# Output stores issued by ScalarE, one value load behind the x transposes, one key load a weight slice later: a linear-attention and SwiGLU kernel on one Trainium2 core

## Chip, cores and metric

The kernel runs on one NeuronCore of one Trainium2 chip. The metric is the device time of one execution in microseconds (us). Before the change the median of 5 runs is 329.17 us (328.5 to 330.03).

## The reference: what is computed

Eight batches, eight heads, 576 tokens, head size 64. Attention is linear (cosFormer): a feature map `phi` doubles the head size, and keys are summed against values once per head, so that no matrix of 576 by 576 arises. The result is normalised (RMS) and goes through a gated FFN of width 1536.

```python
def phi(x, c, s):                       # c, s: cos and sin of pi/2 * pos / 576
    r = np.maximum(x, 0.0)
    return np.concatenate([r * c, r * s], axis=-1)
kv  = np.einsum('bhsf,bhsd->bhfd', phi(k), v)
z   = np.sum(phi(k), axis=2)
x   = np.einsum('bhsf,bhfd->bhsd', phi(q), kv) / (phi(q) @ z + 1e-06)
x   = x.transpose(0, 2, 1, 3).reshape(8 * 576, 512)
xn  = x / np.sqrt(np.mean(x * x, -1, keepdims=True) + 1e-06) * rms_g
g   = xn @ w_gate                       # 512 -> 1536
out = (g * sigmoid(g) * (xn @ w_val)) @ w_out
```

Inputs and output are float32; the matmuls run in bfloat16.

## The kernel before

**Blocks and steps.** The 4608 rows of x are cut into nine blocks of 512. Block b below 8 holds the first 512 tokens of batch b; block 8 holds the last 64 tokens of all batches. A block has twelve gate/value steps n = 0 to 11 (`gval_step`: eight matmuls of 512 columns, a Silu on ScalarE, a product on VectorE, L426, L435, L441), and then four output steps j = 0 to 3 (`out_step`, numbered n = 12 to 15: twelve matmuls of 512 columns into one of two PSUM banks psC, and then `out_store`). Gate and value banks psG and psV are two each, in turn.

**What lies between.** The attention of the next batch is done inside the steps of the running block. A call `at(blk, n, where, f, ...)` puts work into a step; `run` emits it at the places "pe" (ahead of the step's matmuls), "mid", "pre" (ahead of the Silu or of the output copy) or "post" (behind it). So the order on every engine and queue is written out by hand: each engine takes its instructions in the order in which they are emitted, and an instruction that has to wait holds up all that is behind it on its engine. For batch nb, in block nb - 1:

- `k_phi`, `q_phi` (L209 on ScalarE, L211 on VectorE): the feature maps. `v_cast` (L265): values to bfloat16, in a lower and an upper half.
- `kvz_pe` (L282): keys against values; needs `k_phi` and both halves of `v_cast`.
- `nd_pe`, `nd_post`, `x_sq`, `x_norm` (L310, L364, L375, L387): numerator and denominator, division, RMS.
- `x_tr_dma` (L406): a transpose of x by DMA, issued by SyncE (SP), from the tile xn into xnT, which the next block's matmuls read. `q_tr_dma` (L246) does the same for q.

**Loads.** `load_piece` brings k, v and q of batch nb in block nb - 2, in pieces of 288 KB (k, v) or 256 KB (q), and all of them are issued by SP. Batch 3 differs: its k comes in steps 0 to 3 of block 1, its q in 6 to 10, its v in 10 to 13. The weights are loaded by GpSimd at the start, in slices that `weight_dmas` holds in the order gate, value, gate, value and so on: entry 4 is the gate slice and entry 5 the value slice of columns 512 to 768, entry 8 the gate slice of columns 1152 to 1536. The k of batch 1 waits for an entry of that list, and its `k_phi` runs in steps 6 to 10 of block 0.

**Stores.** `out_store` copies a PSUM bank to SBUF (tile osb, four buffers) and issues its store to HBM. In blocks 1 to 8 ScalarE makes the copy and SP issues the store (L456; in block 8 two stores of 64 rows each, L460).

Of the kernel before, what the change touches and what calls it, by code (L numbers as in the profile page):

```python
# [13 lines left out]
SYNC_DEP = mybir.DependencyInfo(mybir.DependencyClass.Sync, mybir.DependencyReason.DATA)  # L14
# [9 lines left out]
def kernel(  # L24
# [11 lines left out]
    nc = tc.nc  # L36
# [27 lines left out]
    V, A, G = nc.vector, nc.scalar, nc.gpsimd  # L64
# [6 lines left out]
    def load_kv(which, b, r0=0, r1=4, j0=0, j1=NJ):  # L71

        key = (which, b)
        if key not in raw:
            raw[key] = (two if which == "k" else one).tile(
                [P, 4, NJ * D], FP32, name=f"r{which}", tag=f"r{which}"
            )
        src = {"k": k, "v": v}[which]
        return nc.sync.dma_start(
            out=raw[key][:, r0:r1, j0 * D : j1 * D],  # L80
            in_=src[b, 2 * r0 : 2 * r1, :, :]
            .rearrange("h s d -> (h s d)")
            .rearrange("(r p n) -> p r n", p=P, n=NJ * D)[:, :, j0 * D : j1 * D],
        )

    def load_q(b, h0=0, h1=8):
        key = ("q", b)
        if key not in raw:
            raw[key] = one.tile([P, H, 4 * D], FP32, name="rq", tag="rq")
        return nc.sync.dma_start(  # L90
            out=raw[key][:, h0:h1, :],
            in_=q[b, h0:h1, 0:512, :].rearrange("h (p j) d -> p h (j d)", j=4),
        )

    def load_q_tail(b):
        t = four.tile([P, 4, D], FP32, name="rqt", tag="rqt")
        raw[("qt", b)] = t
        for g in range(2):
            d = nc.sync.dma_start(
                out=t[64 * g : 64 * g + 64, :, :],  # L100
                in_=q[b, 4 * g : 4 * g + 4, 512:576, :].rearrange("h s d -> s h d"),
            )
        return d
# [9 lines left out]
    def load_q_tokens(b, j0, j1):  # L113
# [45 lines left out]
        out=th[:, 0:NC_], in0=fidx[:, :], scalar1=ang, scalar2=None, op0=ALU.mult  # L159
    )  # L160
    for c0, c1, less in ((4, 5, 64.0), (5, NC_, float(S))):
        nc.vector.tensor_scalar(
            out=th[64:128, c0:c1], in0=fidx[64:128, c0:c1], scalar1=-less, scalar2=ang,
# [3 lines left out]
        out=th[:, NC_ : 2 * NC_], in0=th[:, 0:NC_], scalar1=math.pi / 2.0, scalar2=math.pi,  # L167
# [93 lines left out]
    def copy(eng, o, i):  # L261
        if eng is nc.scalar:
            nc.scalar.copy(out=o, in_=i)  # L263
        else:
            eng.tensor_copy(out=o, in_=i)  # L265
# [185 lines left out]
    def out_store(eng, blk, j, bank):  # L451
        osb = four.tile([P, DM], FP32, name="osb", tag="osb")
        copy(eng, osb[:, :], bank)
        if blk < 8:
            rows = out[blk * S : blk * S + 512, :].rearrange("(p j) m -> p j m", j=4)
            nc.sync.dma_start(out=rows[:, j, :], in_=osb[:, :])  # L456
        else:
            for i in range(2):
                r0 = (2 * j + i) * S + 512
                nc.sync.dma_start(  # L460
                    out=out[r0 : r0 + 64, :], in_=osb[64 * i : 64 * i + 64, :]
                )

# [25 lines left out]
    weight_dmas = []  # L489
# [142 lines left out]
    def none():  # L632
        return {"pe": [], "mid": [], "pre": [], "post": []}
# [3 lines left out]
    def at(blk, n, where, f, *args):  # L637
        slots.setdefault((blk, n), none())[where].append((f, args))
# [3 lines left out]
            f(*args)  # L642

    d = load_kv("k", 1)
    tc.add_manual_dep(d.ins, weight_dmas[4].ins.name, SYNC_DEP, reason="after most weights")
    gate_q = load_q(1)
    tc.add_manual_dep(
        gate_q.ins, weight_dmas[8].ins.name, SYNC_DEP, reason="after the gate weights"
# [7 lines left out]


    for j in range(NJ):
        at(0, 6 + j // 2, "post", k_phi, V, 1, j, 0)
        at(0, 6 + j // 2, "post", k_phi, A, 1, j, 1)  # L660
    at(0, 10, "post", q_phi, V, 1, 0, 0)
    at(0, 11, "post", q_phi, A, 1, 0, 1)

# [1 line left out]
    for nb in range(2, B):  # L665
        b = nb - 1
# [24 lines left out]
        for j in range(4):  # L691
            n = nds[j]
# [12 lines left out]
    for nb in range(3, B):  # L705

        b = nb - 2
        for i, which in enumerate(("k", "v", "q")):
            for p in range(5 if which == "q" else 4):
                n = (0, 10, 6)[i] + p if b == 1 else 5 * i + p  # L710
                at(b + n // 16, n % 16, "post", load_piece, which, nb, p)

    def gval_step(blk, n, bank=None):
# [8 lines left out]
    def out_step(blk, j):  # L722
        n = 12 + j
        run(blk, n, "pe")
        bank = psC[j % 2][:, :]
        for i in range(NNT):
            if i == NNT // 2:
                run(blk, n, "mid")
            out_mm(blk, j, i, bank)
        run(blk, n, "pre")  # L730
        out_store(nc.scalar, blk, j, bank)
        run(blk, n, "post")
# [12 lines left out]
    for n in range(NNT - 2):  # L745
# [15 lines left out]
        if n == 3:  # L761
            d = load_q_tail(0)
# [11 lines left out]
        if n in nd_at:  # L774
            j = nd_at[n]
# [7 lines left out]
    for j in (2, 3):  # L783
        for n in (NNT - 2, NNT - 1):
            out_mm(0, j, n, banks0[j])
    out_store(V, 0, 2, banks0[2])
    out_store(A, 0, 3, banks0[3])
    for j in (0, 1):
        for n in (NNT - 2, NNT - 1):
# [37 lines left out]
    osb = four.tile([P, DM], FP32, name="osb", tag="osb")  # L827
    for (c0, c1), bank in (((0, 384), psC[1]), ((384, 512), psG[0])):
# [6 lines left out]
        for i in range(2):  # L835
            r0 = (6 + i) * S + 512
            (nc.sync if i == 0 else A).dma_start(
                out=out[r0 : r0 + 64, c0:c1], in_=osb[64 * i : 64 * i + 64, c0:c1]
# [31 lines left out]
```

## Time and profile before

| | |
|---|---|
| median of 5 runs | 329.17 us (328.5 to 330.03) |
| the profiled execution's own time | 329.32 us |
| its span, first to last instruction | 327.5 us |
| TensorE (PE) busy | 315.5 us, 96% |
| VectorE (DVE), ScalarE (ACT), GpSimd (POOL) busy | 186.1, 176.8, 32.1 us |
| mean DMA traffic over the span | 165 GB/s |
| output stores issued by SP, 256 KB each | 32, median 2.6 us to landing |

The profile is one execution. It gives for each engine the time that it was busy, the chain of work that ended last, the waits with what ended them, and each instruction with its start and length. PE is matmul and PEld the weight load beside it; SPq and ACTq are the instructions with which SP and ScalarE issue DMAs, and their length is the issue, not the transfer. In a timeline the columns are the start in us, the length in us, engine, source line, operation, out<-in, the shapes and the count; idle time of the engine ahead of it and what ended that stand in square brackets. A matmul's line can be short of a record, so a step of exactly twice the usual one isn't a wait.

### The profile page before, as it was taken

How to read it: one execution, taken by the hardware profiler on the slowest of the kernel's cores; microseconds unless marked ns; L12 is line 12 of the kernel's file. 1: busy time of each engine (PE TensorE's matmuls, PEld its weight loads, DVE VectorE, ACT ScalarE, POOL GpSimd, SP SyncE). 2: the span in 40 equal slices, each digit the busy share in tenths (PEclk: the TensorE clock that was granted, in tenths of full speed). 3: DMA queues.
4: the chain of work that ended last, by engine and by line, in shares of the span. 5: the costliest groups of instructions: out<-in, count | busy, mean ns of one | idle time of the engine just before them, and what ended most of it. 6: DMA issues, size and time to landing. Idle time of an engine off the chain costs nothing.

```text
span 327.5 us, 6404 instructions
## 1 busy us (share of the span) xinstructions
PE 315.5 (96%) x2406; PEld 160.8 (49%) x2441; DVE 186.1 (57%) x412; ACT 176.8 (54%) x366; POOL 32.1 (10%) x67
## 2 busy tenths in 40 slices
PE   6899999999998999999999999999999999999994
PEld 2488465554444444544454445444544444444442
DVE  6775768787755766578257745773577133203310
ACT  6865775965674457645654576556644233223321
POOL 1660112001100100011001100110011000000000
PEclk9999999999999999999999999999999999999999
DMA  7999999899989665975596569957621400020014
GB/s 255 233 191 267 320 185 333 301 171 220 220 212 220 150 188 167 217 208 164 179 223 194 150 196 210 199 167 215 127 46 32 130 32 0 31 99 1 0 34 96
DMA packets 80337, 53.91 MB, mean 165 GB/s; under 512 B 51377, under 2 KB 67761, under 8 KB 80306
## 3 DMA queue, kind: packets, MB, share of 16 engines
q1 hardware_dynamic: 73264, 48.64, 57.8%
q0 software_dynamic: 6880, 4.72, 9.9%
q8 instruction: 19, 0.31, 0.4%
q10 hardware_dynamic: 162, 0.13, 0.1%
q14 instruction: 12, 0.10, 0.1%
HBM read 37.75 MB, written 9.44 MB: 144 GB/s over the span
## 4 chain that ended last, share of the span: by engine, by line
PE 90%; DMA 3%; ACT 2%; DVE 2%; issue 1%; SPq 0%; ACTq 0%; DVEq 0%
PE psC L446 26%; PE psG L426 26%; PE psV L426 26%; PE psA L282 3%; DMA rv<-in_v_dram 3%; PE psA L310 2%; PE psG L446 1%; PE psG L565 1%; PE psV L565 1%; PE psO L565 1%; ACT kpm L209 1%; PE psC L830 1%; PE psV L254 1%; ACT sg L435 0%; PE psA L317 0%
## 5 line engine op out<-in xcount | busy, mean ns | idle before, releaser
L441 DVE TENSOR_TENSOR hT<-psV,sg 128x512 bf16<-128x512 f32 x102 | 70.4, 690 | 95.1 <-PE psV L426 71.2
L435 ACT ACTIVATE sg<-psG 128x512 f32<-128x512 f32 x102 | 60.6, 595 | 65.2 <-PE psG L426 64.0
L426 PE MATMUL psV<-xnT,wv 128*128 128x512 bf16 (+1 forms) x365 | 92.1, 374 | 0.4
L426 PE MATMUL psG<-xnT,wg 128*128 128x512 bf16 (+1 forms) x352 | 90.9, 374 | 0.7
L446 PE MATMUL psC<-wo,hT 128*128 128x512 bf16 x382 | 88.2, 379 | 0.7
L426 PEld LDWEIGHTS <-wv 128*128 128x128 bf16 x416 | 40.7, 98 | 47.4
L446 PEld LDWEIGHTS <-hT 128*128 128x128 bf16 x420 | 40.2, 98 | 46.7
L426 PEld LDWEIGHTS <-wg 128*128 128x128 bf16 x416 | 38.5, 98 | 41.0 <-DVE xnT L265 0.4
L263 ACT COPY osb<-psC 128x512 f32<-128x512 f32 (+1 forms) x33 | 19.2, 582 | 40.2 <-PE psC L446 38.9
L380 POOL TENSOR_TENSOR rs<-ms,mhalf 128x1 f32<-128x1 f32 x36 | 19.9, 552 | 200.7 <-ACT scr L375 200.7
L387 DVE SCALAR_TENSOR_TENSOR xn<-xt,rs,gb 128x512 bf16<-128x512 f32 x36 | 26.8, 746 | 17.1 <-POOL rs L380 17.1
L375 ACT ACTIVATE scr<-xt 128x513 bf16<-128x513 f32 x36 | 22.8, 634 | 22.6 <-DVE xt L364 22.4
L209 ACT ACTIVATE kpm<-rk,tab 128x256 bf16<-128x256 f32 (+1 forms) x78 | 32.0, 478 | 1.8 <-DMA rk<-in_k_dram 1.8
L364 DVE TENSOR_TENSOR xt<-psA,rec 128x512 f32<-128x512 f32 x35 | 24.2, 691 | 1.2
L211 DVE TENSOR_SCALAR kpm<-rk,tab 128x256 bf16<-128x256 f32 (+1 forms) x84 | 22.3, 329 | 2.3 <-DMA rk<-in_k_dram 2.3
L209 ACT ACTIVATE qp<-rq,tab 128x512 bf16<-128x512 f32 x32 | 22.4, 713 | 0.1
L211 DVE TENSOR_SCALAR qp<-rq,tab 128x512 bf16<-128x512 f32 x32 | 15.4, 494 | 0.4 <-DMA rq<-in_q_dram 0.4
L310 PEld LDWEIGHTS <-qpT 128*128 128x128 bf16 x248 | 11.6, 98 | 6.7 <-issue 0.3
L310 PE MATMUL psA<-kvzs,qpT 128*128 128x65 bf16 x248 | 12.8, 193 | 0.3
L282 PEld LDWEIGHTS <-kpm 64*128 64x128 bf16 x576 | 10.0, 95 | 5.1 <-issue 4.0
L426 PE MATMUL psG<-xnt_tail,wg 128*128 128x512 bf16 x48 | 12.3, 379 | 0.1
L426 PE MATMUL psV<-xnt_tail,wv 128*128 128x512 bf16 x47 | 12.1, 379 | 0.0
(89 smaller groups left out, 166.8 us busy)
## 6 DMA issues: line engine op xcount, KB each, us to landing
out_dram<-osb SPq DMA_DIRECT2D x32, 256.0 KB, 2.6
rv<-in_v_dram SPq DMA_DIRECT2D x21, 288.0 KB, 3.2
rk<-in_k_dram SPq DMA_DIRECT2D x20, 288.0 KB, 3.6
rq<-in_q_dram SPq DMA_DIRECT2D x20, 256.0 KB, 3.2
rk<-in_k_dram SPq DMA_DIRECT2D x2, 1152.0 KB, 8.9
rq<-in_q_dram SPq DMA_DIRECT2D x2, 1024.0 KB, 8.5
rv<-in_v_dram SPq DMA_DIRECT2D x3, 576.0 KB, 8.4
wo<-in_moe_w_out_dram POOLq DMA_DIRECT2D x4, 384.0 KB, 6.9
```

Of the source, the lines that this page charges most:

```text
L209: nc.scalar.activation(out=out_ap, in_=in_ap, func=AF.Relu, scale=scale)
L211: eng.tensor_scalar(out=out_ap, in0=in_ap, scalar1=scale, scalar2=0.0, op0=ALU.mult, op1=ALU.max)
L282: nc.tensor.matmul(banks[c][:, r * E : (r + 1) * E], lhsT=kp_main[b][lo : lo + 64, j, r, :], rhs=vvm[b % 2][lo : lo + 64, r, j, :], start= ...
L310: nc.tensor.matmul(o[:, g, i, :], lhsT=qpT[(b, 0)][:, h, j * P : (j + 1) * P], rhs=kvz_of(b, h), start=True, stop=True,)
L364: nc.vector.tensor_tensor(out=xt[:, 0:DM].rearrange("p (b h d) -> p b h d", b=2, d=D), in0=o[:, :, :, 0:D], in1=rec[:, :, :].unsqueeze(3). ...
L375: nc.scalar.activation(out=scr[:, :], in_=xt[:, 0 : DM + 1], func=AF.Square, scale=1.0 / math.sqrt(DM), accum_out=ms[:, :],)
L380: nc.gpsimd.tensor_tensor(out=rs[:, :], in0=ms[:, :], in1=mhalf[:, :], op=ALU.pow)
L387: nc.vector.scalar_tensor_tensor(out=xn[:, :], in0=x_of[(b, j)][:, 0:DM], scalar=rs_of[(b, j)][:, :], in1=gb[:, :], op0=ALU.mult, op1=ALU. ...
L426: nc.tensor.matmul(pst[bank][:, cols[0] : cols[1]], lhsT=w[:, t, n * P : (n + 1) * P], rhs=x[:, t, cols[0] : cols[1]], start=(t == 0), sto ...
L435: nc.scalar.activation(out=sg[:, :], in_=psG[bank][:, :], func=AF.Silu)
L441: nc.vector.tensor_tensor(out=hTs[blk][:, n, :], in0=psV[bank][:, :], in1=sg[:, :], op=ALU.mult)
L446: nc.tensor.matmul(bank, lhsT=hTs[blk][:, n, j * P : (j + 1) * P], rhs=wo[:, n, :], start=(n == 0), stop=(n == NNT - 1),)
```

## The change

The stores of blocks 1 to 8 are issued by ScalarE in place of SP. All four pieces of v of batch 3 are issued at the end of step 13 of block 1, where the last two x transposes of batch 2 are already emitted, in place of one in each of the steps 10 to 13. The k of batch 1 waits for weight entry 5 in place of 4, and its nine pairs of `k_phi` go from 2, 2, 2, 2, 1 in steps 6 to 10 to 3, 2, 2, 2 in steps 7 to 10.

```diff
@@ out_store
         if blk < 8:
             rows = out[blk * S : blk * S + 512, :].rearrange("(p j) m -> p j m", j=4)
-            nc.sync.dma_start(out=rows[:, j, :], in_=osb[:, :])
+            (nc.scalar if blk else nc.sync).dma_start(out=rows[:, j, :], in_=osb[:, :])
         else:
             for i in range(2):
                 r0 = (2 * j + i) * S + 512
-                nc.sync.dma_start(
+                nc.scalar.dma_start(
                     out=out[r0 : r0 + 64, :], in_=osb[64 * i : 64 * i + 64, :]
                 )
@@ batch 1
     d = load_kv("k", 1)
-    tc.add_manual_dep(d.ins, weight_dmas[4].ins.name, SYNC_DEP, reason="after most weights")
+    tc.add_manual_dep(d.ins, weight_dmas[5].ins.name, SYNC_DEP, reason="after most weights")
...
     for j in range(NJ):
-        at(0, 6 + j // 2, "post", k_phi, V, 1, j, 0)
-        at(0, 6 + j // 2, "post", k_phi, A, 1, j, 1)
+        at(0, 7 + max(0, j - 1) // 2, "post", k_phi, V, 1, j, 0)
+        at(0, 7 + max(0, j - 1) // 2, "post", k_phi, A, 1, j, 1)
@@ load pieces of batches 3 to 7
         for i, which in enumerate(("k", "v", "q")):
             for p in range(5 if which == "q" else 4):
-                n = (0, 10, 6)[i] + p if b == 1 else 5 * i + p
+                n = (p, 13, 6 + p)[i] if b == 1 else 5 * i + p
                 at(b + n // 16, n % 16, "post", load_piece, which, nb, p)
```

## The prediction

> **What bounds the kernel now.** First the page: which engine is full, and what the chain of work that ended last is made of.
>
> ```profile
> PE 315.5 (96%) x2406; PEld 160.8 (49%) x2441; DVE 186.1 (57%) x412; ACT 176.8 (54%) x366; POOL 32.1 (10%) x67
> PE 90%; DMA 3%; ACT 2%; DVE 2%; issue 1%; SPq 0%; ACTq 0%; DVEq 0%
> ```
>
> TensorE sets the time, and SP's queue has no measurable share of the chain. So a change of queues can gain only where PE stands still for a transfer. The list of waits and PE's timeline show where it stands still. From 18.2 us, when the FFN matmuls begin, to 322.7 us there is one such place of over 0.6 us, in block 2, at the keys-against-values of batch 3.
>
> ```profile
> 97.99 0.75 PE L282 MATMUL psA<-vvm,kpm 64*128 64x65 bf16 x36
> 99.97 0.76 PE L282 MATMUL psA<-vvm,kpm 64*128 64x65 bf16 x36 [1.23 <-DVE vvm L265]
> 98.17 0.69 DVE L441 TENSOR_TENSOR hT<-psV,sg 128x512 bf16<-128x512 f32 x1 [0.64 <-PE psV L426]
> 98.77 0.48 DVE L211 TENSOR_SCALAR qp<-rq,tab 128x512 bf16<-128x512 f32 x1
> 99.17 0.76 DVE L265 CAST vvm<-rv 128x1152 bf16<-128x1152 f32 x1
> ```
>
> This looks like a late v, but isn't: the cast of v's upper half follows VectorE's product of step 3 and a q_phi back to back, and the product had to wait for PE itself (0.64). v had landed long before: the last piece was issued at 89.18 us and took 4.0 us, so it was there at 93.2. The 1.2 us is VectorE's written order, which the change leaves alone. The other candidate is the start of block 2 (PE from 90.99 us), which needs the last x transpose of batch 2. SP's timeline, and the landing of the transpose issued at 86.71:
>
> ```profile
> 82.25 1.27 SPq L99 DMA_DIRECT2D rqt<-in_q_dram  x2
> 83.57 0.60 SPq L79 DMA_DIRECT2D rv<-in_v_dram  x1
> 84.27 1.23 SPq L406 DMA_TRANSPOSE xnT<-xn  x1
> 85.60 0.54 SPq L456 DMA_DIRECT2D out_dram<-osb  x1
> 86.19 0.41 SPq L79 DMA_DIRECT2D rv<-in_v_dram  x1
> 86.71 1.39 SPq L406 DMA_TRANSPOSE xnT<-xn  x1
> ...
> DMA to landing us min/median/max: 3.8/3.8/3.8
> ```
>
> Store and v pieces stand between the transposes; the last one lands at 86.71 + 3.8 = 90.5, 0.5 us ahead of its need, and PE shows no gap there. All later x transposes land early (block 2: issued at 118.53, landed after 2.5, needed at 126.3).
>
> **What the Trainium skill says.** "DMA: Bandwidth & Descriptors", section "Issuing engines are not separate DMA queues": DMAs from SP and ScalarE run on the same 16 engines, and issuing from both saves only sequencer time. The trace fits, as the chain gives SPq 0%. "Perfetto Trace Analysis", section "DMA Instruction — HWDGE (DVE, Sync)": an issue holds the sequencer while it waits for the lock of a descriptor generator that the sequencers share, generates, and pushes its semaphore; that whole window is in the profile. Before, hardly anything but SP uses it, so no wait for the lock shows here; it is the unknown of this change.
>
> **Part 1: 34 stores from SP to ScalarE** (28 in blocks 1 to 7, 6 halves in block 8). ScalarE's price is visible once, at the end:
>
> ```profile
> 322.73 0.48 ACT L263 COPY osb<-psC 128x384 f32<-128x384 f32 x1 [1.36 <-PE psC L830]
> 323.24 0.55 ACTq L837 DMA_DIRECT2D out_dram<-osb  x1
> 323.83 0.27 ACT L263 COPY osb<-psG 128x128 f32<-128x128 f32 x1 [0.62 <-PE psG L830]
> ```
>
> From the end of one copy to the next instruction it is 0.62 us; the overlap with the next instruction that is lost (0.1) makes it 0.72. Below, it can't be under the 0.33 of SP's shortest store; above, behind one transpose in the generator (1.2) it is 0.7 + 1.2 = 1.9. I take 0.72. In all 34 x 0.72 = 24 us on ScalarE, which is busy 177 of 327.
>
> Is it hidden? Behind each store wait ScalarE's x_sq and k_phi, and, behind the block's last one, the Silu that frees a PSUM bank for PE. The tightest place is the end of block 1:
>
> ```profile
> 88.60 0.59 ACT L263 COPY osb<-psC 128x512 f32<-128x512 f32 x1 [0.67 <-PE psC L446]
> 89.08 1.30 ACT L209 ACTIVATE kpm<-rk,tab 128x256 bf16<-128x256 f32 x3
> 90.29 0.62 ACT L375 ACTIVATE scr<-xt 128x513 bf16<-128x513 f32 x1
> 91.19 0.59 ACT L263 COPY osb<-psC 128x512 f32<-128x512 f32 x1 [0.19 <-PE psC L446]
> 92.05 0.60 ACT L435 ACTIVATE sg<-psG 128x512 f32<-128x512 f32 x1 [0.28 <-PE psG L426]
> ```
>
> The first store of the block fits into the 0.80 in which ScalarE waits for xt. The second's 0.72 meets 0.67 of idle: 0.05 late. The third adds 0.72, less 0.19; the fourth 0.72, less 0.28. So the Silu of step 0 comes about 1.0 late, ends at 93.65, and PE wants its bank again in step 2, at 94.44 (from PE's timeline): 0.8 us to spare. Steps of 1.73 us with Silu and q_phi spaced 0.5 + 0.6 catch up within two steps. In the output steps of blocks 2 to 6, idle times of 0.8 to 1.3 per step absorb more; block 7 has 2.0 per step. In block 8 a copy and two issues take 0.59 + 2 x 0.6 = 1.8 of a step's 2.6; the last two end near 322.6, the next copy is due at 322.73. On the path: 0. If prices are p, the lateness at block 2 is 2p + (p - 0.67) - 0.47, and it reaches PE when it passes 1.8, from p = 0.98.
>
> A store also waits on ScalarE for its copy (its own engine, 0.03 seen above) and for the landing of the eighth DMA before it, as the records hand out eight completion semaphores in turn: for the last store of block 1 that is the first, 8 us older and landed by then. 0.
>
> SP gains: its stores no longer wait for copies ahead of loads and transposes. What was held up there was early or, at 86.71, 0.5 ahead, so nothing on the path.
>
> **Part 2: v of batch 3 behind the transposes.** No instruction more or less; two pieces leave the space ahead of the last two transposes, a third that between, and the four now follow them. The transpose issued at 86.71 goes at about 86.5, when its x_norm (85.72 + 0.75) is done, and lands after about 2.5 to 3 (the x transposes' median is 2.5, against 3.8 and 4.3 here): near 89.3, 1.7 ahead of its need in place of 0.5. No PE time, as none was lost. The v pieces go from 87.8 to 90.2 and, at the 3.3 to 4.5 us seen, land from 91.5 to 94.7. The casts that read them start at 95.71 and 99.17, in VectorE's order: 2 us or more to spare. What follows them on SP is a tail transpose that block 8 needs, and q transposes from 94.2. 0; at worst, should four pieces beside two stores land 2 us later, 0.3.
>
> **Part 3: k of batch 1.** Gate slice 4 was issued at 14.09 and value slice 5 at 14.82; by their landings (7.4 and 8.0 us) they are there at 21.5 and 22.8. So k leaves 1.3 later, and after its 10.3 lands near 33.1 in place of 31.8. Its first k_phi on ScalarE was at 31.96, 0.2 behind the landing:
>
> ```profile
> 31.96 0.90 ACT L209 ACTIVATE kpm<-rk,tab 128x256 bf16<-128x256 f32 x2
> 33.20 0.60 ACT L435 ACTIVATE sg<-psG 128x512 f32<-128x512 f32 x1 [0.34 <-PE psG L426]
> ```
>
> It moves behind the Silu at 33.20, to 33.69: margin 0.6. Three k_phi (1.3) fit before the Silu at 34.92. In step 10 VectorE has one k_phi more (0.3) ahead of q_phi; its product then comes about 0.1 late, against a PE stall of 0.1 that ScalarE sets there. Weights 6 to 9 share the bandwidth with k a little less; no matmul waits for them before. q of batch 1 waits for slice 8 as before, and v follows it on SP; their casts have some 0.8 of margin. GpSimd's next weights wait for q and move with it. 0, between -0.1 and +0.2.
>
> **The sum.** 0 + 0 + 0 against the profiled execution's 329.32 (span 327.5 and 1.8 around it), which lies 0.15 over the median of 329.17. Half a tenth of a per cent may come from the wider margins in executions that lose them; I take 0.2 us off the median: **328.9**. About 0.3% (1.0 us) is what a measurement of this kernel can tell from no change.
>
> **Rivals.**
> *The margins are lost in ordinary executions.* For it: 0.5 us at the transpose and 0.2 at k are thin, and the runs spread over 1.5 us. A transpose that needs the longest landing seen (q's, 5.7) would come 1.9 later and cost PE 1.4; the fix then gives all of it. Against it: the profiled execution was slower than the median without any such stall. Time: 327.9, within 327.4 to 328.2.
> *ScalarE's issues hold up the Silu (slower).* Place: the end of block 1 and the start of block 2. If transposes and stores queue for the generator (1.2 us each, twice in these steps), the price passes 0.98; at p = 1.3 the lateness is 2.8 and PE stops for 1.0, giving 330.2. Should p be 1.3 in every block, blocks 3 to 7 would lose some 0.5 each, and more than 332. Against it: among loads and transposes SP's stores took 0.33 to 0.65.
> *v too late (slower).* From a landing after 95.7 or 99.2 the cast waits and PE's 1.2 grows by as much: 330. Needs 1 to 4 us more than the landings show.
> That the change doesn't do what it says could be so in part 2 alone, if the pieces were still held by something older on SP; nothing there is.
>
> **How the numbers follow.** No change that counts 0.44 (328.2 to 330.1, most likely 328.9); margins 0.36; slower by ScalarE 0.16, by v or k 0.04. The range takes in the margins' case and ScalarE's at 1 us: 327.5 to 330.4. Faster 0.36, same 0.44, slower 0.20.
>
> **What would show it.** Right: ACTq L456 with some 0.5 us each, the last x transpose of batch 2 landing before 90, PE's 1.2 at 99 still there, and no gap of PE at the start of blocks 2 to 8. Wrong: a PE wait on ScalarE's sg or DVE's hT two steps into a block, ACTq lines over 1 us, a cast or k_phi that waits for its DMA, or a span shorter by over 1 us.

## The result, and the profile after

Median of 28 runs: **328.8 us** (328.45 to 332.04). The kernel before, on the same chip: 328.95 us (47 runs, 328.44 to 330.98). The ratio is 0.9995, with a 95% interval of 0.9983 to 1.0007: no change. The lowest times of the two differ by 0.01 us.

The profiled execution of the kernel after took 330.05 us, span 328.3, 0.8 more than the span before. First it has to be seen where that comes from. Page of the kernel after: engines, the granted clock by slices, and the chain.

```profile
PE 317.5 (97%) x2406; PEld 162.3 (49%) x2441; DVE 185.7 (57%) x412; ACT 177.7 (54%) x366; POOL 31.9 (10%) x67
PEclk9799999999999999999999999999999999999999
PE 91%; ACT 3%; DVE 2%; issue 1%; DMA 1%; ACTq 0%; DVEq 0%
```

PE is busy 2.0 us longer with the same 2406 instructions, and the second slice of the clock shows a 7. Windows of 2 us around it, kernel after (start:end, length, then busy time and count of PE, PEld, DVE, ACT, POOL, and at the end the granted clock, DMA share, GB/s):

```profile
8.00:10.00 2.00, 2.00 (x6) 0.51 (x5) 2.00 (x8) 2.00 (x6) 0.23 (x1) 0.83 1.04 375
10.00:12.00 2.00, 2.00 (x23) 1.79 (x23) 1.52 (x3) 1.28 (x3) 2.00 (x3) 0.50 1.17 283
12.00:14.00 2.00, 1.94 (x76) 1.77 (x72) 0.60 (x4) 0.93 (x3) 2.00 (x4) 0.82 1.40 180
```

The middle window of the kernel before:

```profile
10.00:12.00 2.00, 1.72 (x52) 1.44 (x53) 1.76 (x5) 1.60 (x3) 1.04 (x2) 1.00 1.02 289
```

At half the clock PE got through 23 matmuls there in place of 52. No instruction of the change runs this early, and an execution of the unchanged kernel has a like clock and span (b_again below: mean clock 0.993, span 328.1). So spans of single profiles can't be compared here. What can be compared are distances inside the trace. I cut at two PE instructions: the first output matmul of block 0 (L446) and the first FFN matmul of block 2 (L426).

| kernel | start to block 0's output | from there to block 2 | block 2 to the end | mean clock |
|---|---|---|---|---|
| before | 40.77 | 50.22 | 236.5 | 1.000 |
| after | 41.57 | **50.22** | **236.5** | 0.992 |

Behind the opening, the two executions agree to the hundredth of a microsecond up to block 2, and to the tenth after it. The other profiles of this document say the same of the opening: it took 39.95 to 40.77 us in the seven with a mean clock of 0.997 or more, and 41.41 to 43.70 us in the five with 0.993 or less (store3 and k_7 left aside, the one because its clock fell later, the other because its edit stops PE in the opening). Beneath that equality several things moved. PE's timeline of the kernel after, block 2:

```profile
91.79 1.03 PE L426 MATMUL psG<-xnT,wg 128*128 128x512 bf16 x4
...
98.80 0.75 PE L282 MATMUL psA<-vvm,kpm 64*128 64x65 bf16 x36
100.78 0.75 PE L282 MATMUL psA<-vvm,kpm 64*128 64x65 bf16 x36 [1.23 <-DVE vvm L265]
```

All of it is 0.8 later than before, PE's stop of 1.23 included, which stays exactly as long. Now the two queues that the change works on, SP and ScalarE, at the end of block 1:

```profile
84.01 4.46 SPq L406 DMA_TRANSPOSE xnT<-xn  x2
88.52 2.20 SPq L79 DMA_DIRECT2D rv<-in_v_dram  x4
```

```profile
86.94 0.56 ACT L263 COPY osb<-psC 128x512 f32<-128x512 f32 x1
87.53 0.34 ACTq L456 DMA_DIRECT2D out_dram<-osb  x1
87.92 1.31 ACT L209 ACTIVATE kpm<-rk,tab 128x256 bf16<-128x256 f32 x3 [0.42 <-ACT osb L263]
...
92.23 0.56 ACT L263 COPY osb<-psC 128x512 f32<-128x512 f32 x1
92.82 0.34 ACTq L456 DMA_DIRECT2D out_dram<-osb  x1
93.21 0.60 ACT L435 ACTIVATE sg<-psG 128x512 f32<-128x512 f32 x1 [0.41 <-PE psG L426]
```

On SP nothing stands between the two transposes any more, and the four v pieces follow them. On ScalarE each copy is followed by an issue of 0.34. But the last transpose, issued at 87.28, landed after 4.1 us, at 91.34: not sooner than before (3.8), though v was taken out of its way. That is the number to explain. Its view, the landing of that one instruction in the kernel after:

```profile
L406 SPq DMA_TRANSPOSE xnT<-xn x1: 1192/1192/1192, 87.3 to 87.3; - x1
DMA to landing us min/median/max: 4.1/4.1/4.1
```

### The profile page after: what moved, and what is told of

Read it like the earlier page. It is cut to its first block, busy times and chain, and to the rows that moved or that the text cites. A ratio compares the mean times of both kernels' runs of the same rounds, so it can differ in the third digit from the quotient of the medians.

```text
span 328.3 us, 6386 instructions
## 1 busy us (share of the span) xinstructions
PE 317.5 (97%) x2406; PEld 162.3 (49%) x2441; DVE 185.7 (57%) x412; ACT 177.7 (54%) x366; POOL 31.9 (10%) x67
## 4 chain that ended last, share of the span: by engine, by line
PE 91%; ACT 3%; DVE 2%; issue 1%; DMA 1%; ACTq 0%; DVEq 0%
PE psC L446 26%; PE psG L426 26%; PE psV L426 26%; PE psA L282 3%; PE psA L310 2%; PE psG L446 1%; ACT kpm L209 1%; DMA rk<-in_k_dram 1%; PE psG L565 1%; PE psV L565 1%; PE psO L565 1%; PE psV L254 1%; PE psC L830 1%; PE psO L254 1%; ACT sg L435 0%
## 5 line engine op out<-in xcount | busy, mean ns | idle before, releaser
L426 PE MATMUL psV<-xnT,wv 128*128 128x512 bf16 (+1 forms) x365 | 92.1, 374 | 0.4
L426 PE MATMUL psG<-xnT,wg 128*128 128x512 bf16 (+1 forms) x352 | 90.9, 374 | 0.7
L446 PE MATMUL psC<-wo,hT 128*128 128x512 bf16 x382 | 88.2, 379 | 0.7
L426 PEld LDWEIGHTS <-wv 128*128 128x128 bf16 x416 | 40.7, 98 | 47.4
L446 PEld LDWEIGHTS <-hT 128*128 128x128 bf16 x420 | 40.3, 98 | 46.6
L426 PEld LDWEIGHTS <-wg 128*128 128x128 bf16 x416 | 38.5, 98 | 41.0 <-DVE xnT L265 0.4
L263 ACT COPY osb<-psC 128x512 f32<-128x512 f32 (+1 forms) x33 | 19.2, 580 | 32.5 <-PE psC L446 31.1
L426 PE MATMUL psG<-xnt_tail,wg 128*128 128x512 bf16 x48 | 12.3, 379 | 0.1
L426 PE MATMUL psV<-xnt_tail,wv 128*128 128x512 bf16 x47 | 12.1, 379 | 0.0
```

The source lines that it names most:

```text
L426: nc.tensor.matmul(pst[bank][:, cols[0] : cols[1]], lhsT=w[:, t, n * P : (n + 1) * P], rhs=x[:, t, cols[0] : cols[1]], start=(t == 0), sto ...
L446: nc.tensor.matmul(bank, lhsT=hTs[blk][:, n, j * P : (j + 1) * P], rhs=wo[:, n, :], start=(n == 0), stop=(n == NNT - 1),)
```

## The experiments

The theory of the prediction: all three parts are off the critical path. Rivals: two parts with effects of opposite sign cancel; the gain lies in executions that no profile caught. Each kernel is compared with runs of the kernel before on the same chip; "lowest" is the fastest of its runs.

### The parts alone: p_store, p_v, p_k

```diff
p_store, against before:
-            nc.sync.dma_start(out=rows[:, j, :], in_=osb[:, :])
+            (nc.scalar if blk else nc.sync).dma_start(out=rows[:, j, :], in_=osb[:, :])
...   (and L460: nc.scalar)
p_v, against before:
-                n = (0, 10, 6)[i] + p if b == 1 else 5 * i + p
+                n = (p, 13, 6 + p)[i] if b == 1 else 5 * i + p
p_k, against before: weight_dmas[5], and k_phi in steps 7 to 10, as in the change
```

> The kernel before with the stores of blocks 1 to 8 issued by ScalarE, and nothing else. Main theory (a store issue on ScalarE costs 0.5 us and is hidden below 0.98): no change, within 0.3 us of before; the Silu of step 0 of block 2 some 0.3 us late, no gap of PE at the block starts. A theory in which the parts cancel (stores lose what v or k gains): slower by 0.5 us or more. In the trace I expect the last x transpose of batch 2, now beside a store on another queue and not ahead of it, to take 4 us to its landing.

> The kernel before with v of batch 3 in step 13 behind the x transposes, stores still on SP. Main theory: no change, within 0.3 us. If the transposes were slowed by the v pieces, the last one lands within 3 us of its issue (1.5 us ahead of PE's need); if it is the stores that slow it, it stays near 3.8. The theory that thin margins are lost in ordinary runs expects a gain of 0.5 us or more in the median.

> The kernel before with k of batch 1 behind weight entry 5 and its k_phi one step later, and nothing else. Main theory: no change, within 0.3 us; k lands near 32 to 33 us, ahead of its first k_phi on ScalarE by 0.5 us or more. The theory of lost margins expects a gain; a theory in which the later k delays q and v of batch 1 expects a loss of 0.5 us at 41 to 46 us.

Measured, with 329.94 (lowest 328.54, 51 runs) for before on this chip: p_store 329.63, lowest 328.98, ratio 1.0002 (0.9979 to 1.0024); p_v 329.0, lowest 328.50, 0.9977 (0.9964 to 0.9991); p_k 329.08, lowest 328.52, 0.998 (0.9965 to 0.9995).

The medians hide what the trace of **p_store** shows. PE's timeline has a gap at the start of block 2 that neither before nor after has:

```profile
88.73 5.35 PE L446 MATMUL psC<-wo,hT 128*128 128x512 bf16 x24
94.59 1.02 PE L426 MATMUL psG<-xnT,wg 128*128 128x512 bf16 x4 [0.50 <-DMA xnT<-xn]
```

In **p_v** the stores are still on SP, behind the transpose (SP's timeline, and the landing of the transpose):

```profile
86.10 1.20 SPq L406 DMA_TRANSPOSE xnT<-xn  x1
87.42 0.50 SPq L456 DMA_DIRECT2D out_dram<-osb  x1
87.96 2.20 SPq L79 DMA_DIRECT2D rv<-in_v_dram  x4
```

```profile
L406 SPq DMA_TRANSPOSE xnT<-xn x1: 1195/1195/1195, 86.1 to 86.1; - x1
DMA to landing us min/median/max: 2.4/2.4/2.4
```

2.4 us: about the value that the prediction had taken for the whole change (2.5 to 3). The transpose was there at 88.5, and PE began block 2 at 90.60, a margin of 2.1. So v's move does all that was expected of it only as long as the stores stay on SP. **p_k**: k landed at 32.34, the first k_phi on ScalarE began at 33.12, and nothing waits for it. From block 0's output to block 2, p_v has 50.23 and p_k 50.22, from there to the end 236.5 and 236.6: as before. Their ratios lie 0.2% below one, with intervals that leave one out; taken by the numbers, the margins theory had expected such gains. But no wait of PE is gone in either trace, and the lowest times are those of before. The odd figure is 329.94: in the other comparisons the kernel before had medians of 328.95, 329.22 and 329.27, and kernels that keep both thin margins, at the transpose and at k, had 329.12 and 329.06 on the other chip (b_again and store_not1). So the 0.2% lies more likely in those 51 runs than in the two edits. That isn't shown.

### The stores again, and before against itself: p_store_2, b_again

p_store's profile had a clock of 0.987, so the same kernel was run again beside a second copy of the kernel before.

> The stores of blocks 1 to 8 on ScalarE alone, a second time, for a look at full clock. In the first look the last x transpose of batch 2 took 5.2 us to its landing and PE stopped for 0.7 us at the start of block 2. New theory (on its own queue a store no longer queues behind the transposes but runs beside them and slows them): the gap of 0.4 to 0.7 us is there again, and the time is 0.3 to 0.6 us over before. Old theory (the store is hidden, nothing moves): no gap, the first look was a disturbed one.

> The kernel before, unchanged, against itself: what the comparison shows when nothing differs, and a second look at where its runs differ. Main theory: ratio 1.000, its runs spread over 1.5 us or more, by the granted clock and the first transfers of the opening, with the x transpose of batch 2 in time. The theory of lost margins expects a gap of PE at the start of block 2 in a run at full clock that is a microsecond late.

Measured, with 329.22 (lowest 328.53, 59 runs) for before: p_store_2 330.06, lowest 329.14, 1.0008 (0.9985 to 1.0032); b_again 329.12, lowest 328.50, 0.9996 (0.9979 to 1.0014). p_store_2's profile has a clock of 1.000, and the gap is there (PE's timeline, and the landing of the transpose):

```profile
88.25 2.32 PE L446 MATMUL psC<-wo,hT 128*128 128x512 bf16 x10
90.95 1.02 PE L426 MATMUL psG<-xnT,wg 128*128 128x512 bf16 x4 [0.38 <-DMA xnT<-xn]
```

```profile
L406 SPq DMA_TRANSPOSE xnT<-xn x1: 1188/1188/1188, 85.9 to 85.9; - x1
DMA to landing us min/median/max: 5.0/5.0/5.0
```

From block 0's output to block 2 it is 50.76, 0.54 more than the 50.22 of before (and 0.67 more in p_store's trace); the lowest time is 0.61 up, and was 0.44 up for p_store. The intervals of the ratios are wider than that and take in no change, but two traces and two lowest times say the same, and 14 runs of the kernel before (b_again) have a lowest time that isn't up: **the stores alone cost about half a microsecond.** b_again's trace has 41.41, 50.22 and 236.5 at clock 0.993: the kernel before with the opening of the profile after.

### Where the half microsecond arises: store_not1

```diff
against before:
+            (nc.scalar if blk > 1 else nc.sync).dma_start(out=rows[:, j, :], in_=osb[:, :])
```

> The kernel before with the stores of blocks 2 to 8 on ScalarE, those of block 1 still on SP. If the loss of the stores alone is the two stores of block 1 that run beside the last two x transposes of batch 2, it is gone: no gap of PE at the start of block 2, time as before within 0.2 us, fastest run near 328.5. If the loss is ScalarE's time in every block, some 0.5 us remain.

329.06, lowest 328.63, against 329.27 and 328.62 (47 runs): 1.0004 (0.9975 to 1.0032). The last transpose of batch 2 landed after 3.5 us, block 2 begins without a gap, 50.22 after block 0's output:

```profile
92.10 1.03 PE L426 MATMUL psG<-xnT,wg 128*128 128x512 bf16 x4
```

So 30 of the 34 stores cost nothing that is seen (the lowest time is 0.01 up), and the loss sits in the stores of block 1, which are issued beside the last transposes. The landing of the last x transpose of batch 2, over the kernels:

| stores of block 1 | v pieces | landed after, us | margin to PE, us |
|---|---|---|---|
| SP | behind the transposes (p_v, b_v_cast) | 2.4, 2.4 | 2.1 |
| SP | between (before, b_again, b_cast, store_not1, p_k) | 3.8, 4.0, 3.9, 3.5, 3.5 | 0.45 to 0.9 |
| ScalarE | behind (after, a_cast, k_7, v_late) | 4.1, 4.2, 4.1, 4.2 | 0.3 to 0.46 |
| ScalarE | between (p_store, p_store_2) | 5.1, 5.0 | none, PE waits |

The table has both signs. With the stores on either engine, v's move is worth 0.8 to 1.6 us of landing; with v in either place, the stores' move costs 1.0 to 1.8. On SP the store that becomes ready during the transpose goes out behind it (87.42 in p_v). On ScalarE it goes out at once, 0.25 us after the transpose has started to be issued (87.53 and 87.28 in the kernel after). That the store on ScalarE is what delays the transpose is shown. That it does so by going out earlier, and not by being on another queue, is the reading; no run held a store back on ScalarE. Nor do these runs tell whether the two then share the generation of descriptors or the transfer.

The later blocks, where no v piece stands near, bear the effect out. The last x transpose of batch 5, issued in block 4, has a store 1.30 us behind its own issue on SP in the kernel before, and 0.35 us behind it on ScalarE in the kernel after. The landing, before and then after:

```profile
L406 SPq DMA_TRANSPOSE xnT<-xn x1: 1197/1197/1197, 185.9 to 185.9; - x1
DMA to landing us min/median/max: 2.6/2.6/2.6
```

```profile
L406 SPq DMA_TRANSPOSE xnT<-xn x1: 1190/1190/1190, 186.7 to 186.7; - x1
DMA to landing us min/median/max: 4.3/4.3/4.3
```

It is so with the last x transpose of each of the batches 3 to 7: 2.4 to 2.7 us in the six profiles with these stores on SP, 3.5 to 4.5 us in the seven with them on ScalarE (store3 left aside), store_not1 among them. There the delay costs nothing, because the transpose has time: the one of batch 5 lands at 190.9 in the kernel after, and PE needs it at 194.46. Block 1 is only the place where the margin is thin.

### What does stop PE: a_cast, b_cast, b_v_cast

The one stop of PE, 1.23 us, was read as VectorE's order. The cast of v's upper half goes one step earlier, into step 2:

```diff
a_cast against after; b_cast against before; b_v_cast against before, with p_v's edit as well:
-        at(vb, vn + 1 + (nb == 3), "post", v_cast, V, nb, *HIGH)
+        at(vb, vn + 1, "post", v_cast, V, nb, *HIGH)
```

> The changed kernel with the cast of the upper half of v of batch 3 one step earlier (step 2 of block 2 in place of 3). Main theory: PE's stop of 1.2 us in block 2 is VectorE's written order, so it goes: faster by 1.2 us than before, near 327.7, ratio 0.996. Rival: the stop stands for a late v; then the cast waits for its transfer on VectorE, the products behind it are late, and the time stays at before's within 0.3 us. The last piece of v landed 1.5 us ahead of where the cast would now start.

> The kernel before with the cast of the upper half of v of batch 3 in step 2 of block 2 in place of 3, and nothing else. Main theory (PE's stop of 1.2 us is VectorE's written order, and v is there anyway): faster by 1.2 us, ratio 0.996. If the new place of the v loads is what makes the earlier cast pay, this one stays within 0.3 us of before.

> The kernel before with v of batch 3 in step 13 and its upper cast in step 2, stores still on SP and k as before. Main theory: 1.2 us faster than before (ratio 0.996), as fast as the same cast in the changed kernel, so that neither the stores on ScalarE nor the later k are needed; the last x transpose lands within 3 us. If stores on ScalarE have a worth of their own, it stays 0.3 us or more behind that kernel.

| kernel | median | lowest | ratio to before | before: median, lowest |
|---|---|---|---|---|
| a_cast | 327.46 | 327.13 | 0.9914 (0.9889 to 0.994) | 329.94, 328.54 |
| b_cast | 328.48 | 327.07 | 0.9967 (0.9951 to 0.9984) | 329.22, 328.53 |
| b_v_cast | **327.52** | 327.10 | 0.9945 (0.9929 to 0.9961) | 329.22, 328.53 |

The lowest times are 1.4 us down in all three. VectorE's and PE's timelines of b_v_cast, where the two groups of 36 matmuls have become one of 72 with no wait:

```profile
96.61 0.48 DVE L211 TENSOR_SCALAR qp<-rq,tab 128x512 bf16<-128x512 f32 x1
97.00 0.75 DVE L265 CAST vvm<-rv 128x1152 bf16<-128x1152 f32 x1
97.73 0.69 DVE L441 TENSOR_TENSOR hT<-psV,sg 128x512 bf16<-128x512 f32 x1
```

```profile
97.55 1.33 PE L282 MATMUL psA<-vvm,kpm 64*128 64x65 bf16 x72
```

The cast no longer stands behind the product that waits for PE. From block 2 to the end it is 235.15 us in place of 236.5, so the gain lies behind the start of block 2, where this was PE's only stop of its size. b_v_cast beats both the kernel before and the kernel after. That it beats b_cast isn't shown: their intervals overlap, and the lowest times are equal. a_cast, which has the stores on ScalarE and the later k as well, is no faster (its ratio is taken against the high median of 329.94), so neither of these two is needed.

### ScalarE's price pushed up: store3

Here each store of 512 columns becomes three, on ScalarE, to find the point from which ScalarE's issues reach PE.

```diff
against after:
-            (nc.scalar if blk else nc.sync).dma_start(out=rows[:, j, :], in_=osb[:, :])
+            if blk:
+                for c0, c1 in ((0, 192), (192, 384), (384, 512)):
+                    nc.scalar.dma_start(out=rows[:, j, c0:c1], in_=osb[:, c0:c1])
+            else:
+                nc.sync.dma_start(out=rows[:, j, :], in_=osb[:, :])
```

> The changed kernel with each store of blocks 1 to 7 cut into three by columns (192, 192, 128), all on ScalarE: the issue's price goes from 0.5 to about 1.25 us. By the prediction's sum (2p + (p - 0.67) - 0.47 late, PE stops past 1.8) block 2 starts 0.8 us late, and blocks 3 to 6 by 0.5 to 0.7 each: slower by about 3 us (2 to 5), with waits for sg two steps into a block. If ScalarE goes on while an issue is under way, nothing moves: within 0.3 us of the changed kernel.

348.23 us (346.8 to 348.99, four runs), ratio 1.0562 (1.0529 to 1.0594): 19 us, far more than expected. ScalarE's and PE's timelines, block 1 into 2:

```profile
87.03 1.71 ACTq L458 DMA_DIRECT2D out_dram<-osb  x3
88.78 1.30 ACT L209 ACTIVATE kpm<-rk,tab 128x256 bf16<-128x256 f32 x3 [1.79 <-issue]
90.00 0.56 ACT L263 COPY osb<-psC 128x512 f32<-128x512 f32 x1
91.50 1.62 ACTq L458 DMA_DIRECT2D out_dram<-osb  x3
93.17 1.31 ACT L209 ACTIVATE kpm<-rk,tab 128x256 bf16<-128x256 f32 x3 [2.61 <-DMA rv<-in_v_dram]
...
97.59 1.18 PE L426 MATMUL psG<-xnT,wg 128*128 128x512 bf16 x4 [2.52 <-ACT sg L435]
98.57 1.91 PE L426 MATMUL psV<-xnT,wv 128*128 128x512 bf16 x4
100.27 1.76 PE L426 MATMUL psG<-xnT,wg 128*128 128x512 bf16 x4
```

The place is the one that the prediction named for its slower rival: PE waits for the Silu's bank in step 2. The price is not 1.25. Three issues hold ScalarE 1.3 to 1.8 us, and at least six of them first wait for older DMAs. The prediction had named that wait and put it at nothing: eight completion semaphores go in turn over the DMAs of SP and ScalarE together, so each DMA waits for the eighth before it. With three times the stores, the eighth before it is young. The first issue of the second group could go at 90.6 and went at 91.50, when the x transpose of 86.77 had landed (91.42); the second went at 92.30, when the v piece of 88.02 had landed (92.28). In the kernel after, none of ScalarE's stores waits so. PE stops by 2.7, 2.0, 3.7, 3.2 and 2.9 us in step 2 of blocks 2 to 6 (from start to start of two matmuls, less the usual 0.216; the view's 2.52 is the idle time), and after three of these stops, as here, about seven matmuls run at 0.43 us spacing in place of 0.216. That is 14.5 and some 3 x 7 x 0.21 = 4.4, against the 19.2 by which the part from block 2 to the end is longer (255.7 in place of 236.5). So there is a limit, made of the issues and of the eight semaphores together, and one store per step is well inside it.

### k and v pushed on: k_7, v_late

```diff
k_7 against after:
-    tc.add_manual_dep(d.ins, weight_dmas[5].ins.name, SYNC_DEP, reason="after most weights")
+    tc.add_manual_dep(d.ins, weight_dmas[7].ins.name, SYNC_DEP, reason="after most weights")
v_late against after:
-                n = (p, 13, 6 + p)[i] if b == 1 else 5 * i + p
+                n = (p, 15, 6 + p)[i] if b == 1 else 5 * i + p
```

> The changed kernel with k of batch 1 behind weight entry 7 in place of 5. k leaves near 26 and lands near 35 to 36, past its first k_phi (33.7 to 34.5). ScalarE and VectorE wait for it 1 to 2 us; PE has 1.8 us of room, so no change or up to 0.5 us slower. A loss of over 1 us would say that the margin at k is the tight one.

> The changed kernel with v of batch 3 in step 15 of block 1 in place of 13. Issued some 4 us later, the pieces land near 97 to 100; the lower cast is due at 95.7 to 96.5, the upper at 99.2 to 100. The prediction's threshold says that VectorE then waits for its transfer and PE's 1.2 us at keys-against-values grow by 1 to 3 us: slower by 1.5 us. If VectorE's order alone sets that stop, nothing moves.

**k_7**: 330.81, lowest 329.62, against 329.27 and 328.62: 1.0037 (1.0018 to 1.0055), +1.0 in the lowest, more than expected. ScalarE's and PE's timelines:

```profile
36.28 1.30 ACT L209 ACTIVATE kpm<-rk,tab 128x256 bf16<-128x256 f32 x3 [3.26 <-DMA rk<-in_k_dram]
37.49 0.57 ACT L435 ACTIVATE sg<-psG 128x512 f32<-128x512 f32 x1
38.12 1.02 PE L426 MATMUL psG<-xnT,wg 128*128 128x512 bf16 x4 [1.41 <-ACT sg L435]
```

k left at 26.88 and landed at 36.26; ScalarE stood 3.26 for it, with a Silu behind the k_phi. The Silu came 3.35 later than its place in the rhythm of the steps, PE 1.58 late: 1.8 us are swallowed. That is the room the prediction read from PE's timeline for block 2 (two PSUM banks, a step of 1.73), here confirmed in block 0.

**v_late** tells nothing about v. SP issues nothing in steps 14 and 15 that v could fall behind, so every engine's order is that of the kernel after, and the run is a repeat of it: 328.97, lowest 328.54, 0.9985 (0.9968 to 1.0001). From which lateness v would hurt was not tried.

## Why the prediction was right, and where not

The number was right (328.9 forecast, 328.8 measured), and so was the sum for the whole change: nothing on the path. In part that was luck: of the three zeros, the stores' was wrong by half a microsecond, and v's move, which alone brings the last transpose to 2.4 us, made up for it at the same place. The steps:

- **PE's one stop is VectorE's order: right.** 1.23 before, 1.23 after, gone with the cast one step earlier.
- **ScalarE's price, 0.72 a store: too high.** In blocks 1 to 7 the issue is 0.34 to 0.40, the idle ahead of the next instruction, issue included, 0.42; with the lost overlap of 0.1, some 0.5. (The halves of block 8 take 0.47 to 0.61 each, where 0.6 was said.) Taken back to the time of before, the Silu of block 2's step 0 starts at 92.41 (93.21 - 0.80) against 92.05, so 0.36 late, where 1.0 was worked out; with 0.5 the prediction's formula gives the same 0.36. Either price is inside the 1.8 of room. One reading beside it was off: the third output steps of blocks 2 and 4 have 0.19 of idle on ScalarE, not 0.8 to 1.3. No harm came of it.
- **A wait for a generator shared with SP**, which the Trainium skill describes ("Perfetto Trace Analysis", section "DMA Instruction — HWDGE (DVE, Sync)") and the slower rival needed: not seen in the kernel after. ScalarE's issue at 87.53 lies wholly inside SP's transpose of 87.28 to 88.47, and took 0.34. In store3 it can't be ruled out: the second and third issues of a store took mostly 0.44 to 0.46 where SP issued nothing, and mostly 0.50 to 0.67 beside an issue of SP.
- **"On the path: 0" for the stores: this step failed.** It priced the stores where they went, on ScalarE, and looked at SP only for what gets shorter. It did not ask what the stores' place on SP had been good for: there they were behind the transpose. Alone they cost 0.5, through the last x transpose. The skill's sentence that issuing from two engines saves only sequencer time ("DMA: Bandwidth & Descriptors", section "Issuing engines are not separate DMA queues") was read as "and costs nothing", and SPq 0% in the chain as agreement. The runs of p_store refute that reading, not the section, which says in the same place that DMAs from several engines interleave.
- **The transpose lands after 2.5 to 3, margin 1.7: wrong for the whole change** (4.1, margin 0.46), right for v's part alone (2.4, margin 2.1). The issue time was right: 86.48 in the time of before, where 86.5 was said. By the prediction's own list this was a sign that it didn't bear out: a landing before 90, where it was 90.54 in that time. The zero came out because the two errors meet at this transpose.
- **v: right in effect, landing mis-sized.** The pieces took 5.4 to 6.5 us, not 3.3 to 4.5; the last was there at 96.78, and its cast began at 99.97. The lower half had 1.8 to spare.
- **k: right.** It landed at 32.16, 2.3 ahead of ScalarE's first k_phi at 34.49 (33.1 and 33.69 were forecast). It left at 21.72, 0.25 later than in the profile before, and 1.0 later in p_k, where 1.3 was said. PE shows no wait for the gate and value weights.
- **The margins rival** explained the spread of the runs by lost margins. The traces don't bear it out: what differs between executions of one kernel, as far as profiles caught it, lies in the opening. b_again's profile, 0.8 us over the median of its runs at a clock of 0.993, has the transpose in time. The theory isn't excluded for executions that no profile caught, and p_v's 0.2% could be its remainder.

## What to carry to other kernels

A DMA queue is also an order. Whoever moves a transfer to another engine's queue should list what it stood behind there, for that will now run beside it: here a store of 256 KB that had waited behind a transpose cost it 1.0 to 1.8 us of landing, and PE half a microsecond in the one place where the margin was thinner than that. Where a large rearrangement measures as zero, run its parts alone, and compare distances between two instructions inside the traces rather than spans. And when PE waits for a cast, look first at what stands ahead of the cast on its own engine: one line moved there gave more than all transfers together.

## What was not expected of the hardware

- In the profile after, the granted clock went down to 0.50 from 10 to 12 us, and to 0.83 and 0.82 beside it; the opening was 0.8 us longer. The kernel before shows a like opening in b_again (41.41 in place of 40.77, mean clock 0.993).
- Even at a clock of 1.000 the opening differs: 40.77 in before and 39.95 in b_cast, whose instructions up to there are the same.
- In store3, matmuls of 512 columns ran at half rate for some 3 us after three of PE's five stops (2.7, 3.7 and 2.9 us) and not after the two others (2.0 and 3.2). The granted clock was 0.50 from 99.5 to 101.5 us, behind the first of them.
